# Attention and two expert layers on one core: the front of the kernel in a new order, with fewer operations on GpSimd

## The chip, the core and the metric

The kernel runs on one core of a Trainium2 chip. TensorE (PE in the profile) multiplies, VectorE (DVE), ScalarE (ACT) and GpSimd (POOL) work element by element, SyncE (SP) issues the transfers. The metric is the time of one execution in microseconds; lower is better. Most executions agree within 0.3%.

## What is computed

```python
# q, k, v: (2, 8, 576, 64); x: (1152, 512)
mask_plain = (rel >= 0) & (rel < 32)                       # heads 0 to 3
mask_dil = (rel >= 0) & (rel < 128) & (rel % 4 == 0)       # heads 4 to 7
scores = np.where(mask, scale * q @ k.T, -1e9)
attn = np.exp(scores - scores.max(-1, keepdims=True))
x = (attn / (attn.sum(-1, keepdims=True) + 1e-09)) @ v     # 1152 tokens of 512
h = x @ w_in                                               # (512, 1024)
e = np.exp(h - h.max(-1, keepdims=True))
solu = h * e / (e.sum(-1, keepdims=True) + 1e-9)
ln = (solu - mean(solu)) / np.sqrt(var(solu) + 1e-6) * g_ln
x = ln @ w_out                                             # (1024, 512)
p = domain_probs / (domain_probs.sum(-1, keepdims=True) + 1e-09)
for e in range(4):                                         # w1 (4, 512, 1024), w2 (4, 1024, 512)
    out += p[:, e:e + 1] * (np.maximum(x @ w1[e], 0.0) @ w2[e])
```

w_in and w_out arrive as 64-bit floats; everything else has 32 bits.

## The kernel before

**Precision.** A large product is made of three: each operand is split into a high part in the fp32r format and the rest, and high times high, high times low and low times high are added in PSUM. The splits are elementwise work: a copy that rounds (`copy`, on ACT, or on VectorE where the flag `alt` is set), and a subtraction for the low part (`tt` and `pick`, on GpSimd, or on VectorE with `alt`).

**Order by hand.** The first half of the kernel is not a loop. Each job is a generator that issues a few instructions and yields; the text `ORDER` names the jobs one after the other, and each mention advances that job by one step. A `+` behind a name sets `alt` for that step, `*n` puts n matmuls on a tile of zeros (`busy`, L178, the fillers) ahead of the step's own. Each engine does its instructions in the order in which the steps issue them. The jobs:

- lI, lO, lD, lP, lvd, lvp, lW: loads, issued on SP's queue.
- AD and AP: transposes of q and k (L290, L307), for the dilated and the plain heads.
- UD and UP, 12 units (`att_U`): mask and scores (L321, L332), maximum (L338), subtraction (L340), exponent on ACT (L343), sum (L345), plus 1e-9 (L347), reciprocal (L349), product into a padded buffer pd (L353), transposes (L359), copy pt, the product with v (L373), and the split of the result into xhi and xlo (L188 or L190, L275).
- VI and VO: decode of w_in and w_out from 64 to 32 bits (`convert`): the low word scaled on ACT (L204), the magnitude of the high word (L207 on VectorE or L209 on ACT), a clamp (L211), mask and shift (L213), the sign put back (L215), the sum of the two as integers (L217, GpSimd), then the split (L242; with the factor g_ln L258 to L266).
- H.t, 9 token tiles of 128: the first GEMM (24 matmuls of 128x512, L402) and the chain of softmax and normalisation (L407 to L425) with a power on GpSimd (L423).
- T.t: transposes of the result (L439) and their split (L188 or L190, L275 or L452). X.c.dp: the second GEMM, 48 matmuls of 128x384 (L465).
- XQ and WP: sums and splits of x and of the first w1 for a product with 7 instead of 8 multiplications (L496).

**The experts.** After ORDER come 8 half-experts in a loop. `up(0)` (512 tokens) and `up(1)` (640) are 7 products each (L578, 12 matmuls) with additions (L592 to L614), a relu on ACT (L588) and the low part on VectorE (L589). `down` is one step for each of 9 token tiles (L633, 12 matmuls), added to the result with the token's probability (L635, L637). For the first half-expert, `feed` puts the rest of XQ, the next w1 (WP.1) and w2 (WV) behind the products by the texts FIRST and SECOND. down 0 to 3 follow up(1), then up(0) of the next half-expert, then down 4 to 8.

**PSUM.** Two pools of two tiles each, pm and pa. `ptile` picks one by its argument and `alt`, `pair` takes them in turn.

Of the kernel before, what the change touches and what calls it, by code (L numbers as in the profile page):

```python
# [21 lines left out]
ORDER = """
lI.1 lD.0.0 lI.0 lP.0.0 AD.0.0*13 VI.1 VI.1 AD.0.0 VI.0 AP.0.0*24 lI.4 VI.1 lI.3 VI.0 VI.1 lI.2 VI.1 VI.0 lD.1.0
lP.1.0 VI.1 VI.0 AP.0.0 VI.4 VI.0 VI.0 VI.1 lvp.0.0 lO.0.0 VI.4+ VI.1 AD.0.0+*6 AP.0.0*8 VI.4 VI.4 VI.4 AP.0.0
UP.0.0+*6 VI.0+ AD.0.0 VI.3 UP.0.0 VI.0+ VI.4 VI.3 UP.0.0 UP.0.0 lO.0.1 VI.4 VI.3 VI.4 VI.2 VI.3 AD.1.0*30 UP.0.0 VI.3
AD.1.0 lD.0.1 AD.1.0*5 lvd.0 VI.2+ UP.0.0 AD.1.0 VI.3 VI.2 AP.1.0 AP.1.0 UD.0.0*9 UP.0.0 VI.3 VI.2 UP.0.0 lP.2.0 VI.2
UD.2.0 UD.0.0 UP.0.0+ UD.0.0 UD.0.0 UD.2.0 VO.0.0 UD.0.0 UD.1.0+ UP.0.0 UD.2.0 UD.0.0 VI.2 UD.0.0 UD.2.0 AP.1.0+
UD.0.0 AD.0.1+ VI.2+ AP.1.0 UP.0.0+ UD.2.0 VI.2 VO.0.1 UD.1.0 UD.2.0 AD.0.1 UD.1.0 lD.1.1 UD.0.0 UP.0.0 UD.1.0 UP.1.0
UD.2.0 UP.0.0 UD.2.0+ UD.0.0 UD.1.0 lvp.1.0 VO.0.1+ AD.0.1 VI.3 AD.0.1 UP.1.0 misc VO.0.0 UD.2.0+ VO.0.1 UD.1.0
AP.2.0+ UP.1.0 AP.2.0 UD.2.0 VO.0.1 UD.1.0 UD.0.0+ UD.1.0 lP.0.1 AP.2.0+ VO.0.1 AD.1.1+ VO.0.0 AP.2.0+ UP.1.0 UD.2.0+  # L30
AD.1.1 VO.0.1 VO.0.0 AD.1.1+ UP.2.0 UD.0.0 endE UD.2.0 VO.0.0 lO.1.1 UD.0.0 VO.0.1 lvp.2.0 VO.0.0 UP.1.0 UD.2.0 AD.1.1
UP.1.0 UD.1.0+ VO.0.1 UP.2.0 lO.1.0 VO.0.0+ AP.0.1 UP.1.0 UP.2.0 UD.1.1+ lP.1.1 UD.1.0 VO.0.0+ UP.2.0 UP.1.0 UP.2.0
AP.0.1 VO.1.1 UD.1.0+ UD.1.1 VO.1.1 UP.2.0 UP.1.0 UD.1.1 lvd.1 UD.0.1 VO.1.1 UD.1.0 UP.2.0 UD.1.1 UP.2.0 UP.1.0 VO.1.1
UD.1.0 UD.1.1 VO.1.0 AP.0.1+ UP.2.0 AP.0.1 VO.1.1 UD.1.1 AP.1.1+ VO.1.1 UP.2.0 UD.1.1 UD.2.1+ UD.0.1 AP.1.1 VO.1.0+
UD.0.1 VO.1.0 VO.1.0 VO.1.1+ UD.1.1 VO.1.0 lO.2.1 UP.1.0+ lP.2.1 UD.0.1 UD.1.1 UP.1.0 UD.2.1 UP.0.1 VO.1.0 UD.1.1
VO.1.1 UD.2.1 VO.1.0+ lO.2.0 UD.1.1 UP.1.0 UD.0.1 UD.2.1 AP.1.1+ UD.2.1 lvp.0.1 AP.1.1 UD.2.1 UP.2.0+ UD.1.1 UD.2.1
VO.1.0+ H.1 UP.2.0 UD.2.1 UD.0.1 VO.2.1 UD.1.1 VO.2.1 UD.0.1 UP.2.0 UD.0.1 VO.2.1 lvp.1.1 VO.2.1 UP.0.1 VO.2.0 VO.2.0
VO.2.1 UP.0.1 VO.2.1 VO.2.0 UP.0.1 VO.2.0 UP.0.1 VO.2.1 lO.3.1 UP.1.1 VO.2.0 H.1 VO.2.0 UD.2.1 UP.1.1 H.0 H.1 VO.2.1
lO.3.0 UP.0.1 UD.2.1 UP.1.1 UP.0.1 VO.3.1 H.1 UP.0.1 H.1 H.1 VO.3.1 VO.2.0+ VO.3.1 H.1 VO.3.1 UP.1.1 VO.2.0+ VO.3.0
UP.1.1 VO.3.0+ UD.2.1 H.0 UD.0.1 H.1 UD.2.1 UD.2.1 H.1 H.2 H.0 VO.3.1 H.1 UP.1.1 UD.0.1 H.0 H.0 VO.3.1 H.0 H.1+ H.0  # L40
UP.1.1 VO.3.0 VO.3.0 H.0 VO.3.0 VO.3.1 H.0 H.0 AP.2.1 UP.0.1 H.0 AP.2.1 UP.0.1 VO.3.0 VO.3.1+ T.0 T.0+ T.1 T.0 H.3 T.0
VO.3.0 T.1 T.1+ H.2 H.2 H.2 H.2 T.1 VO.3.0 H.2 UP.1.1 AP.2.1 AP.2.1 UP.0.1 H.2 UP.0.1+ lvp.2.1 UP.2.1*1 UP.0.1 UD.0.1
H.2 H.2 UD.0.1 UP.2.1 H.2 H.2+ UP.2.1 UD.0.1 UP.2.1 H.3 UP.1.1 T.2 UP.2.1 UP.1.1 H.4 T.2+ UP.2.1 H.3 H.3 UP.2.1 T.2+
H.3 H.3 T.2 H.3 H.3 UP.2.1+ UP.2.1 X.0.1 H.3 H.4 H.3 H.3 H.4 H.4 H.4 H.4 H.4 H.4 H.4 UP.2.1+ H.4 H.4+ UP.2.1 UP.1.1
UP.2.1+ UP.2.1 X.0.0 UP.1.1 UP.1.1 endA X.0.1+ T.3 X.0.0+ H.5 T.3 T.3 T.3 T.4 H.5 H.6 H.5 T.4+ H.5 T.4+ H.5 H.5 H.5
H.5 H.5 T.4 H.6 H.5 H.5+ T.5 H.6 H.6 H.6 H.6 T.5 H.6 H.7 H.6 T.5 H.6 T.5 H.6 H.6 H.7 H.7 T.6 H.7 H.8 H.7 H.7 T.6 H.7
T.6 H.7 T.6 H.7 X.1.0 H.7 H.8 H.8 H.7 H.8 H.8 H.8 H.8 H.8 H.8 H.8 H.8 T.7 T.7+ X.1.0+ T.7 T.8 X.1.1 T.7 T.8+ T.8+ T.8
endH lW.0 X.1.1 XQ.0 WP.0+ X.2.1 WP.0+ XQ.0+ WP.0 XQ.0+ XQ.0+ WP.0 XQ.0+ WP.0+ X.2.0 XQ.0+ X.2.1 WP.0 XQ.0+ WP.0+
WP.0+ XQ.0 WP.0 XQ.0 WP.0 XQ.0+ XQ.0+ XQ.0+ WP.0 XQ.0+ XQ.0 WP.0+ WP.0+ WP.0+ M X.2.0 XQ.0+ XQ.0 WP.0 M WP.0 WP.0+
WP.0+ M M M M M  # L50
"""
# [4 lines left out]

@with_exitstack
def fused_kernel(ctx, tc, q, k, v, w_in, w_out, g_ln, probs, w1, w2, out):
# [371 lines left out]
    def moe_T(t):  # L430
# [15 lines left out]
        if direct:  # L446
            lo_psum(ll[:, :, cols], pv, lh[:, :, cols])
        else:
            nc.scalar.copy(e, pa)
# [323 lines left out]
```

## Time and profile before

| | us |
|---|---|
| median of three runs | 590.05 |
| lowest, highest | 589.27, 590.79 |
| span of the profiled execution | 588.3 |
| TensorE busy in it | 549.9 (93%) |
| VectorE busy | 381.2 (65%) |
| ACT busy | 198.0 (34%) |
| GpSimd busy | 241.8 (41%) |

Of the profiled execution the span is known and no time of its own beside it. In the chain of work that ended last, 70% of the span is TensorE's and 16% VectorE's. A row of the profile says which line and engine, which operation, out<-in by the program's names, the shapes, how many, busy time and the mean of one in ns, and behind the last bar the idle time before them with what ended it.

### The profile page before, as it was taken

The numbers are of one execution on the slowest core, as the hardware profiler recorded it, in microseconds if no ns is written. First come the engines' busy times: TensorE is split into PE (matmuls) and PEld (weight loads), VectorE is DVE, ScalarE is ACT, GpSimd is POOL, SyncE is SP. The second block draws the span as 40 slices with busy tenths as digits, with TensorE's granted clock in tenths as the row PEclk, the third lists the DMA queues.
The fourth block names the chain that finished last, engine by engine and source line by source line (L and its number), as shares of the span: only waits on it lengthen the run. The fifth ranks groups of instructions, "written<-read, shape, count | busy, mean of one in ns | idle before, by whom it ended". The sixth has DMA issues, their size and how long they took to land.

```text
span 588.3 us, 9316 instructions
## 1 busy us (share of the span) xinstructions
PE 549.9 (93%) x3874; PEld 493.9 (84%) x3874; DVE 381.2 (65%) x506; ACT 198.0 (34%) x306; POOL 241.8 (41%) x178
## 2 busy tenths in 40 slices
...
GB/s 278 268 165 168 139 68 11 10 0 1 1 1 71 144 0 144 1 1 144 0 1 141 3 1 88 57 1 17 127 1 1 143 1 1 71 2 1 0 72 89
DMA packets 33945, 35.80 MB, mean 61 GB/s; under 512 B 18800, under 2 KB 21872, under 8 KB 33520
## 3 DMA queue, kind: packets, MB, share of 16 engines
...
## 4 chain that ended last, share of the span: by engine, by line
PE 70%; DVE 16%; issue 6%; POOL 3%; DMA 2%; ACT 2%; SPq 0%; POOLq 0%; ACTq 0%; DVEq 0%
PE pm L633 17%; PE pa L633 16%; PE pa L578 14%; PE pm L578 13%; PE pm L402 3%; PE pm L465 3%; DVE sw L496 2%; DMA draw<-in_moe_w_in_dram 1%; DVE cva L211 1%; DVE xol L496 1%; DVE lst L407 1%; DVE xlo L275 1%; DVE xoh L188 1%; DVE cva L215 1%; POOL hl L452 1%
## 5 line engine op out<-in xcount | busy, mean ns | idle before, releaser
L589 DVE SCALAR_TENSOR_TENSOR hl<-ct,hh 128x512 fp32r<-128x512 f32 (+1 forms) x64 | 68.4, 1088 | 37.0 <-ACT hh L588 37.0
L578 PE MATMUL pa<-xoh,hh 128*128 128x256 f32 (+1 forms) x192 | 57.8, 301 | 5.2 <-DVE ct L595 3.9
L578 PE MATMUL pm<-xoh,hh 128*128 128x256 f32 (+1 forms) x192 | 58.2, 303 | 4.2 <-DVE ct L595 2.8
L496 POOL TENSOR_TENSOR wl<-wl,wh 128x1024 fp32r<-128x1024 f32 x9 | 22.1, 2451 | 96.3 <-ACT wh L190 96.3
L633 PE MATMUL pm<-wh,hh 128*128 128x512 f32 (+1 forms) x152 | 58.4, 384 | 0.6 <-DVE xf L637 0.6
L588 ACT ACTIVATE hh<-ct 128x512 fp32r<-128x512 f32 (+1 forms) x64 | 42.3, 684 | 49.5 <-DVE ct L610 22.1
L633 PE MATMUL pm<-wl,hh 128*128 128x512 f32 (+1 forms) x152 | 58.3, 384 | 0.0
L633 PE MATMUL pm<-wh,hl 128*128 128x512 f32 (+1 forms) x152 | 58.3, 383 | 0.0
L578 PE MATMUL pm<-xol,hh 128*128 128x256 f32 (+1 forms) x192 | 57.7, 301 | 0.0
L578 PE MATMUL pm<-xoh,hl 128*128 128x256 f32 (+1 forms) x192 | 57.6, 300 | 0.0
L578 PE MATMUL pa<-xol,hh 128*128 128x256 f32 (+1 forms) x192 | 57.4, 299 | 0.0
L578 PE MATMUL pa<-xoh,hl 128*128 128x256 f32 (+1 forms) x192 | 57.3, 299 | 0.0
L633 PE MATMUL pa<-wh,hh 128*128 128x512 f32 x140 | 54.5, 389 | 0.0
L633 PE MATMUL pa<-wl,hh 128*128 128x512 f32 x140 | 54.5, 389 | 0.0
L633 PE MATMUL pa<-wh,hl 128*128 128x512 f32 x140 | 54.5, 389 | 0.0
L496 POOL TENSOR_TENSOR hl<-sw,hh 128x512 fp32r<-128x512 f32 x23 | 35.1, 1526 | 26.6 <-ACT hh L190 8.7
L637 DVE SCALAR_TENSOR_TENSOR xf<-pm,pr,xf 128x512 f32<-128x512 f32 (+1 forms) x33 | 24.1, 730 | 31.8 <-PE pm L633 31.8
L599 POOL TENSOR_TENSOR ct<-ct,ct 128x512 f32<-128x512 f32 (+1 forms) x16 | 23.7, 1481 | 47.9 <-ACT ct L598 46.5
L637 DVE SCALAR_TENSOR_TENSOR xf<-pa,pr,xf 128x512 f32<-128x512 f32 x31 | 23.1, 746 | 30.3 <-PE pa L633 30.3
L578 PEld LDWEIGHTS pa<-xoh,hh 128*128 128x128 f32 x192 | 36.9, 192 | 6.3 <-DVE ct L595 4.2
L578 PEld LDWEIGHTS pm<-xoh,hh 128*128 128x128 f32 x192 | 37.2, 194 | 5.1 <-DVE ct L595 3.0
L190 ACT CAST wh<-wl 128x1024 fp32r<-128x1024 f32 x16 | 16.8, 1054 | 70.7 <-PE pm L633 40.4
...
## 6 DMA issues: line engine op xcount, KB each, us to landing
...
```

The source lines that it names most:

```text
L188: nc.vector.tensor_copy(out, in_)
L190: nc.scalar.copy(out, in_)
L211: nc.vector.tensor_scalar(out=a, in0=a, scalar1=2.0 ** -15, scalar2=122879.9921875, op0=ALU.max, op1=ALU.min)
L402: nc.tensor.matmul(pm[:, n, :], lhsT=xx[:, kk, cols], rhs=ww["in", kk][:, 512 * n:512 * n + 512], start=(kk == 0 and i < 2), stop=(kk == K ...
L465: nc.tensor.matmul(pm[:, dd, 0:CW], lhsT=w_, rhs=x_[:, f, :], start=(f == 0 and i == 0), stop=(f == KF - 1 and i == 2))
L496: pick().tensor_tensor(out=out, in0=a, in1=b, op=op)
L578: nc.tensor.matmul(ps[:, ff, 0:n], lhsT=a[:, kk, fc], rhs=b[:, kk, :], start=kk == 0 and m == 0, stop=kk == 1 and m == 2)
L588: nc.scalar.activation(out=hv, in_=src, func=AF.Relu)
L589: nc.vector.scalar_tensor_tensor(out=lv, in0=src, scalar=0.0, in1=hv.bitcast(F32), op0=ALU.max, op1=ALU.subtract)
L599: nc.gpsimd.tensor_tensor(out=c12, in0=c21, in1=c22, op=ALU.add)
L633: nc.tensor.matmul(po[:, u, 0:dn], lhsT=h_[:, f, cols], rhs=w_, start=(f == 0 and i == 0), stop=(f == 3 and i == 2))
L637: nc.vector.scalar_tensor_tensor(out=acc[:, t, dc], in0=po[:, u, 0:dn], scalar=pr[:, t, e:e + 1], in1=acc[:, t, dc], op0=ALU.mult, op1=ALU ...
```

## The change

ORDER is written anew: no step has fillers, H.0 stands amid the attention units of the first batch, and the first half-expert is part of the text (u.0, u.1, d.0 to d.3, with the loads lV and lW and the steps of XQ.1, WP.1 and WV.0), so FIRST, SECOND and `feed` are gone. What else changes:

- `pick` gives VectorE where it gave GpSimd and the other way round, until `late` is set behind ORDER.
- `convert` takes the magnitude on ACT with a scale of 2^-112, which makes clamp and mask unnecessary; one shift and one sign operation remain on VectorE, and the integer sum goes by `pick`. w_out is always scaled on ACT and its low part made on VectorE.
- `att_U` has three sm and three pd buffers; column 64 of an sm buffer holds 1e-9, so that the sum contains it and L347 falls away.
- `moe_H` keeps maximum, exponent, product with its negative sum, and subtraction of the mean times 1024. What is a factor of a whole token (the softmax's sum, the normalisation) is left out and put into the probabilities `pr` once, in `scales` ("sc"). The sum of squares is made in `moe_T` on ACT; its low part always by VectorE out of PSUM.
- `ptile` chooses the PSUM pool by its argument alone, `pair` by a number that is passed; `up` and `down` are generators.

```diff
 def pick():
-        return nc.vector if alt[0] else nc.gpsimd
+        return nc.gpsimd if alt[0] != late[0] else nc.vector
...
-        pool, tag = (psm, "pm") if main != alt[0] else (psa, "pa")
+        pool, tag = (psm, "pm") if main else (psa, "pa")
...
-        if alt[0]:
-            nc.vector.tensor_scalar(out=au, in0=high.bitcast(U32), scalar1=0x7FFFFFFF, scalar2=None, op0=ALU.bitwise_and)
-        else:
-            nc.scalar.activation(out=a, in_=high.bitcast(F32), func=AF.Abs)
-        yield
-        nc.vector.tensor_scalar(out=a, in0=a, scalar1=2.0 ** -15, scalar2=122879.9921875, op0=ALU.max, op1=ALU.min)
-        yield
-        nc.vector.tensor_scalar(out=au, in0=au, scalar1=0x07FFFFFF, scalar2=3, op0=ALU.bitwise_and, op1=ALU.logical_shift_left)
...
-        nc.gpsimd.tensor_tensor(out=au, in0=au, in1=low.bitcast(U32), op=ALU.add)
+        nc.scalar.activation(out=a, in_=high.bitcast(F32), func=AF.Abs, scale=2.0 ** -112)
+        yield
+        nc.vector.tensor_scalar(out=au, in0=au, scalar1=3, scalar2=None, op0=ALU.logical_shift_left)
...
+        pick().tensor_tensor(out=au, in0=au, in1=low.bitcast(U32), op=ALU.add)
...
-        nc.vector.tensor_reduce(out=st[:, 1], in_=sm, axis=AX.X, op=ALU.add)
-        yield
-        nc.vector.tensor_scalar(out=st[:, 2], in0=st[:, 1], scalar1=1e-9, scalar2=None, op0=ALU.add)
+        nc.vector.tensor_reduce(out=st[:, 2], in_=smx, axis=AX.X, op=ALU.add)
...
+        nc.vector.scalar_tensor_tensor(out=e, in0=e, scalar=-1.0, in1=pm, op0=ALU.mult, op1=ALU.mult, accum_out=nsum[:, t:t + 1])
+        yield
+        if alt[0]:
+            nc.scalar.activation(out=e, in_=e, func=AF.Identity, bias=nsum[:, t:t + 1], scale=-float(DFF))
+        else:
+            nc.vector.tensor_scalar(out=e, in0=e, scalar1=-float(DFF), scalar2=nsum[:, t:t + 1], op0=ALU.mult, op1=ALU.add)
...
+        nc.scalar.activation(out=e, in_=e, func=AF.Square, accum_out=esq[:, t:t + 1])
...
+    def scales():
+        nc.vector.tensor_scalar(out=esum, in0=esum, scalar1=1e-9, scalar2=None, op0=ALU.add)
+        nc.vector.reciprocal(out=nmx, in_=esum)
+        nc.vector.scalar_tensor_tensor(out=esq, in0=esq, scalar=1.0 / DFF ** 3, in1=nmx, op0=ALU.mult, op1=ALU.mult)
+        nc.vector.tensor_tensor(out=esq, in0=esq, in1=nmx, op=ALU.mult)
+        nc.vector.tensor_scalar(out=esq, in0=esq, scalar1=1e-6, scalar2=None, op0=ALU.add)
+        nc.gpsimd.tensor_tensor(out=esq, in0=esq, in1=mhalf, op=ALU.pow)
+        nc.vector.scalar_tensor_tensor(out=nmx, in0=nmx, scalar=1.0 / DFF, in1=esq, op0=ALU.mult, op1=ALU.mult)
+        nc.vector.tensor_tensor(out=pr, in0=pr, in1=nmx.unsqueeze(2).to_broadcast([128, NTT, E]), op=ALU.mult)
```

VectorE's queue before, early in the front, where two tiles of w_in (eva, cva) are decoded while the first unit of attention (sm_340, st_341) runs:

```order
L340 TENSOR_TENSOR sm_340<-pm_301,st_341 128x384
L211 TENSOR_SCALAR eva_338<-eva_338 128x1024
L213 TENSOR_SCALAR eva_338<-eva_338 128x1024
L345 TENSOR_REDUCE st_341<-sm_340 128x6
L215 SCALAR_TENSOR_TENSOR eva_338<-draw3_239,eva_338 128x1024
L207 TENSOR_SCALAR cva_162<-draw2_243 128x1024
L347 TENSOR_SCALAR st_341<-st_341 128x6
L211 TENSOR_SCALAR cva_162<-cva_162 128x1024
L349 RECIPROCAL st_341<-st_341 128x6
L213 TENSOR_SCALAR cva_162<-cva_162 128x1024
```

VectorE's queue now, at the same place, with the units sm0 and sm1 (L326 is the maximum, L328 the subtraction, L333 the sum, L202 the shift, L204 the sign, L231 the low part of w_in, L182 `copy`, L337 the product into pd):

```order
L202 TENSOR_SCALAR eva_323<-eva_323 128x1024
L333 TENSOR_REDUCE st_363<-sm0_112 128x6
L326 TENSOR_REDUCE st_443<-pa_382 128x6
L326 TENSOR_REDUCE st_449<-pa_414 128x6
L231 TENSOR_TENSOR wl0_199<-cva_174,wh0_198 128x512
L328 TENSOR_TENSOR sm1_113<-pa_414,st_449 128x6x64
L333 TENSOR_REDUCE st_352<-sm2_114 128x6
L182 COPY qTp_369<-pm_370 128x2x2x96
L204 SCALAR_TENSOR_TENSOR eva_323<-draw1_272,eva_323 128x1024
L335 RECIPROCAL st_363<-st_363 128x6
L337 TENSOR_TENSOR pd0_109<-sm0_112,st_363 128x6x64
```

Of a decode, two operations are left between those of attention; the low part, a copy out of PSUM and the product into pd have come in.

VectorE's queue before, in up(1) of the first half-expert (L595 to L614 the additions, L589 the low parts, L496 sums of the next w1, L635 the first two down steps):

```order
L595 TENSOR_TENSOR ct1_2297<-pa_2314,ct0_2296 128x640
L496 TENSOR_TENSOR sw1_2291<-sw0_2290,wh6_2147 128x2x256
L602 TENSOR_TENSOR ct0_2296<-pa_2347,ct0_2296 128x640
L589 SCALAR_TENSOR_TENSOR hl1_2142<-ct0_2296,hh1_2141 128x2x320
L606 TENSOR_TENSOR ct1_2297<-pm_2367,ct1_2297 128x640
L496 TENSOR_TENSOR sw2_2292<-wh6_2147 128x2x256
L610 TENSOR_TENSOR ct3_2299<-pa_2385,ct3_2299 128x640
L589 SCALAR_TENSOR_TENSOR hl1_2142<-ct3_2299,hh1_2141 128x2x320
L614 TENSOR_TENSOR ct1_2297<-pm_2403,ct1_2297 128x640
L589 SCALAR_TENSOR_TENSOR hl1_2142<-ct1_2297,hh1_2141 128x2x320
L589 SCALAR_TENSOR_TENSOR hl1_2142<-ct2_2298,hh1_2141 128x2x320
L635 TENSOR_SCALAR xf_1652<-pa_2433,pr_76 128x512
```

VectorE's queue now, in u.1 (L566 to L594 the additions, L558 the low parts, L464 sums and low parts of x and w1, L618 the down steps):

```order
L566 TENSOR_TENSOR ct1_2110<-pm_2127,ct0_2109 128x640
L464 TENSOR_TENSOR xol_1790<-xf_1433,xoh_1789 128x2x320
L464 TENSOR_TENSOR sw3_1964<-xf_1433,sw1_1962 128x640
L618 TENSOR_SCALAR xf_1433<-pm_2156,pr_76 128x512
L182 CAST xoh_1789<-sw3_1964 128x2x320
L464 TENSOR_TENSOR xol_1790<-sw3_1964,xoh_1789 128x2x320
L576 TENSOR_TENSOR ct0_2109<-pm_2171,ct0_2109 128x640
L558 SCALAR_TENSOR_TENSOR hl1_1974<-ct0_2109,hh1_1973 128x2x320
L464 TENSOR_TENSOR hl_1799<-wh6_1937,hh_1798 128x512
L582 TENSOR_TENSOR ct1_2110<-pa_2209,ct1_2110 128x640
L618 TENSOR_SCALAR xf_1433<-pa_2196,pr_76 128x512
L584 TENSOR_TENSOR ct2_2111<-ct1_2110,ct2_2111 128x640
```

The first down steps stand between the products of u.1, and some low parts of x and w1 and one of the additions have come over from GpSimd.

## Rows read from the trace of the kernel before

**Rows 1.** Stretches of the span: engines busy (instructions), PEclk, DMA share, GB/s.

```profile
0.00:112.30 112.30, 89.99 (x1191) 74.17 (x1191) 94.38 (x171) 67.83 (x109) 58.76 (x63) 0.91 0.57 145
8.00:50.00 42.00, 33.49 (x540) 28.48 (x539) 36.17 (x54) 23.09 (x37) 24.91 (x15) 0.80 0.87 210
50.00:92.60 42.60, 35.16 (x481) 28.68 (x481) 40.54 (x82) 31.21 (x55) 19.73 (x19) 0.99 0.47 124
112.30:193.00 80.70, 79.15 (x467) 74.33 (x465) 43.34 (x69) 19.79 (x29) 20.40 (x16) 1.00 0.04 14
193.00:243.20 50.20, 39.41 (x219) 35.85 (x219) 43.91 (x41) 18.41 (x28) 38.98 (x23) 0.90 0.26 85
243.20:588.30 345.10, 341.38 (x2005) 309.55 (x2003) 199.61 (x227) 91.95 (x140) 123.71 (x77) 1.00 0.12 41
```

**Rows 2.** VectorE's instructions by line and form, 0 to 112.3 us.

```profile
L211 DVE TENSOR_SCALAR cva<-cva 128x512 f32<-128x512 f32 x10 | 8.7, 872 | 1.3 <-ACT cva L209 1.3
L213 DVE TENSOR_SCALAR cva<-cva 128x512 uint32<-128x512 uint32 x10 | 7.7, 770 | 0.2
...
L347 DVE TENSOR_SCALAR st<-st 128x6 f32<-128x6 f32 x12 | 6.3, 522 | 0.0
...
L215 DVE SCALAR_TENSOR_TENSOR cva<-cvr,cva 128x512 uint32<-128x512 uint32 x8 | 5.5, 688 | 0.1
...
L353 DVE TENSOR_TENSOR pd<-sm,st 128x384 f32<-128x384 f32 x2 | 2.4, 1185 | 0.0
...
L207 DVE TENSOR_SCALAR cva<-cvr 128x512 uint32<-128x512 uint32 x3 | 1.9, 630 | 0.0
...
L417 DVE TENSOR_SCALAR lst<-lst 128x1 f32<-128x1 f32 x4 | 0.6, 152 | 0.1
...
L188 DVE COPY kTp<-pa 128x384 f32<-128x384 f32 x1 | 0.6, 564 | 0.0
```

**Rows 3.** Timeline of the front: start, duration (us), engine, line.

```profile
25.98 2.77 POOL L217 TENSOR_TENSOR eva<-eva,draw 128x1024 uint32<-128x1024 uint32 x1 [1.16 <-DVE eva L215]
...
26.43 2.35 DVE L347 TENSOR_SCALAR st<-st 128x6 f32<-128x6 f32 x1
...
34.45 0.16 DVE L347 TENSOR_SCALAR st<-st 128x6 f32<-128x6 f32 x1
...
60.34 0.43 DVE L213 TENSOR_SCALAR cva<-cva 128x512 uint32<-128x512 uint32 x1
```

**Rows 4.** GpSimd's integer sums by form, 0 to 112.3 us.

```profile
L217 POOL TENSOR_TENSOR cva<-cva,cvr 128x512 uint32<-128x512 uint32 x8 | 10.6, 1319 | 7.9 <-DVE cva L215 3.0 <-ACT wh L261 1.9 <-ACT xhi L190 1.6
```

**Rows 5.** The chain that ended last: start, duration (us), TensorE's groups.

```profile
112.52 8.33 PE pm L465 x48
...
243.22 1.42 PE pa L578 x12
...
253.17 2.73 PE pm L633 x12
...
266.78 1.76 PE pa L578 x12
```

**Rows 6.** TensorE's waits, 193 to 243.2 us: total, times, longest.

```profile
PE pa L578 <- DVE ct L595: 3.9, 1, 3.9
```

**Rows 7.** VectorE's L589 of 128x512: 193 to 243.2 us, then 243.2 to 588.3.

```profile
L589 DVE SCALAR_TENSOR_TENSOR hl<-ct,hh 128x512 fp32r<-128x512 f32 x4 | 5.8, 1476 | 2.2 <-ACT hh L588 2.2
...
L589 DVE SCALAR_TENSOR_TENSOR hl<-ct,hh 128x512 fp32r<-128x512 f32 x28 | 18.8, 690 | 14.7 <-ACT hh L588 14.7
```

**Rows 8.** The fillers L178 alone, by stretch (TensorE busy, PEld busy, PEclk).

```profile
30.00:50.00 20.00, 0.00 (x0) 0.00 (x0) 0.73 0.70 127
...
sum 60.00, PE 15.29 PEld 11.90; mean PE 3.06 PEld 2.38
```

**Rows 9.** Timeline: a score tile of pa, its matmuls and its maximum.

```profile
70.87 0.34 PE L321 MATMUL pa<-mask,identb 128*128 128x192 bf16 x2
...
75.10 0.54 DVE L338 TENSOR_REDUCE st<-pa 128x6 f32<-128x384 f32 x1
```

More of the change, by code (lines that the diff above doesn't have):

```diff
@@ L28 @@
[L28 to L37, printed above, removed]
@@ L102, in fused_kernel @@
     vd = ap1.tile([128, 3, 4, 2 * D], F32, name="vd", tag="vd")
-    pds = []
-    for i in range(2):
-        pds.append(ap1.tile([128, 2, 480], F32, name=f"pd{i}", tag=f"pd{i}"))
+    pds = [ap1.tile([128, 2, 480], F32, name=f"pd{i}", tag=f"pd{i}") for i in range(3)]
+    sms = [ap1.tile([128, 6, 65], F32, name=f"sm{i}", tag=f"sm{i}") for i in range(3)]
     warmb = ap1.tile([128, 224], BF16, name="warmb", tag="warmb")
@@ L311, in att_AP @@
                 yield
+    unit = {}
+    for b in range(B):
+        for quad, t in (("D", 0), ("P", 0), ("D", 1), ("D", 2), ("P", 1), ("P", 2)):
+            unit[quad, t, b] = len(unit)
     def att_U(quad, t, b):
@@ L444, in moe_T @@
         yield
-        direct = not alt[0]
[L446 to L449, printed above, removed]
-        yield
-        if not direct:
-            nc.gpsimd.tensor_tensor(out=ll[:, :, cols], in0=e.rearrange("p u (f t) -> p (u f) t", t=128), in1=lh[:, :, cols].bitcast(F32),
-                                    op=ALU.subtract)
+        lo_psum(ll[:, :, cols], pv, lh[:, :, cols])
     def moe_X(c, dp):
```

212 lines of the change are left out of this document (99 added, 113 removed).

## The prediction

> **What bounds the kernel now.** I read the table of stretches first [rows 1]. It cuts the span of 588.3 us into three parts. The front, 0 to 112.3 us, is attention, the decode of both weight matrices and the first five H steps; it ends where the second GEMM's first step, X.0.0, starts. There VectorE is busy 94.38 of 112.3 us and GpSimd 58.76, and TensorE shows 89.99 at a mean granted clock of 0.91. Look at 50 to 92.6: VectorE 40.54 of 42.6 us, DMA share 0.47. That is an engine at its limit. Before 50 us it shares the limit with the loads (DMA share 0.87). The middle, 112.3 to 193, is TensorE at 79.15 of 80.7 us with a clock of 1.00: nothing to gain. In the first experts, 193 to 243.2, TensorE works 39.41 of 50.2 us, VectorE 43.91 and GpSimd 38.98. After 243.2 TensorE is busy 341.38 of 345.1 us; the instructions there are the same on both sides.
>
> The first experts show who is late: the list of TensorE's waits names VectorE's adds L595 first [rows 6]. These stand in VectorE's queue behind work that runs slower than it needs to: the split L589 of 128x512 takes 1476 ns there and 690 ns later [rows 7]. The same shows in the front. The addition of 1e-9 to six numbers (L347) took 0.16 us with GpSimd quiet and 2.35 us while GpSimd added 1024 integers (L217) [rows 3]. So GpSimd's work is paid twice, on GpSimd and as stretched work on VectorE.
>
> How much is that in all? Repricing VectorE's rows at the shortest duration of the same form gives about 18 us of stretch in the front and 16.6 in the first experts: L347 at a mean of 522 ns against 160, L213 at 770 against 430 [rows 2, 3], L589 at 1476 against 690, and so on over all forms. That is about 0.35 us of VectorE for each us of GpSimd elementwise work in the front (52 us without the masks of the setup) and 16.6/38.98 = 0.43 in the first experts.
>
> **The change, part by part.** Sums are made against the span of 588.3; the median of 590.05 lies 1.75 us above, which I leave as it is.
>
> *Front, taken from VectorE.* The clamp L211, 8.7 us for ten of 512 words and 2.1 for three of 1024: 10.8. The sign mask L207, five in all: 3.0. L347, 6.3. Four one-column steps of each of the four softmax chains in this part, 16 at 152 ns: 2.4 [rows 2]. Sum 22.5 us.
>
> *Front, put on VectorE.* Integer adds (L217), two of them: no row of before has one on VectorE, so I bound them by L215 of 512 words at 688 ns and by GpSimd's own 1319 [rows 2, 4]; I take the lower, since the other integer form on VectorE lies there: 1.9 us for one of 512 and one of 1024 words, 3.8 at most. Splits of the decoded weights by the form of L215: 2.3 for w_out, 1.9 for w_in. Copies out of PSUM that ACT did: seven query or key tiles and three of xhi at 564 ns [rows 2] or in proportion to their size, and one pt, 7.3 in all. Two more products L353, 0.55 (as a copy of that size) to 1185 ns [rows 2], low end because GpSimd is quieter: 1.1. Setup of a third pair of buffers 1.2. Sum 15.7 us, up to 19.
>
> *Front, stretch.* GpSimd keeps about 28 of its 52 us. What stays on VectorE carries about 8.5 us of the 18 (the rest went with L211, L207 and L347); at 28/52 it is 4.8, so 3.7 less, and I add 2 for new operations that can be held. VectorE's work falls by 22.5 - 15.7 + 1.7 = 8.5 us, with bounds of 3 and 13. The chain of a token tile through the softmax is six steps shorter and loses its visit to GpSimd, and the products no longer wait for a handoff; VectorE's idle 17.9 us falls by perhaps 3. X.0.0 moves forward by about **11 us** (8 to 15). ACT gains w_in's absolute value with its scale and the Square of each tile, and drops as many copies; it was busy 67.83 of 112.3 [rows 1], which covers that. The fillers cost nothing and give back nothing by themselves: 15.29 us of matmuls, all but one in the first 30 us [rows 8], while the DMAs were still bringing inputs.
>
> *Middle.* An X step is 48 matmuls in 8.33 us [rows 5], and TensorE was full. The transposes' lows move from GpSimd to VectorE, which had 37 us free there; the per-token factors are seven short operations that meet nobody before the first down step. Nothing, from -1.5 to +2. SP's queue: the loads of w1 and w2 are issued in the order text rather than behind it, under X steps; the load of the first half-expert has more matmuls ahead of its use than before.
>
> *First experts.* Fourteen products (7 at 1.42, 7 at 1.76) and four down steps at 2.73 are 33.2 us of TensorE [rows 5], against 50.2. Before, the four downs came last, after the waits; now d.0 to d.3 stand between the products of u.1 and fill what these wait for. VectorE needed 43.91 - 16.6 = 27.3 us unstretched and takes over about 2.5 from GpSimd: 29.8. GpSimd falls from 23 instructions of 1.69 us [rows 1] to about 11, 18 us, so the stretch is 16.6 x 18/39 = 7.7. VectorE then needs 37.5 us and stays the later engine, with 1.5 of idle 39 us: **11 us** less (8 to 14; 17 if TensorE's 33.2 is reached).
>
> On that stretch, rows 3 and 7 say only that operations of VectorE stretch while GpSimd runs. The Trainium skill, "SBUF — State Buffer", section "Who interferes with whom", says it is an exclusive lock on a shared port pair, taken by an operation with two SBUF inputs or one in a two-port mode, and that an operation with at most one SBUF input outside those modes is not held. L347 with its one small input was held for 2.35 us, so the trace agrees only if it runs in such a mode. By the rule the new copies out of PSUM are not held at all, I would drop the 2 us added for them and more of the rest, and the sum would come to about 564 as an estimate.
>
> *Afterwards.* The PSUM pools now alternate by a fixed parity and repeat a pool at the seams; the tile that is reused was read two products earlier, and I cost it at nothing. If that cover is gone, up to 0.7 us at each of 14 seams, 10 us.
>
> Sum: 590.05 - 11 - 11 = **568**.
>
> **The rivals.**
> *Both floors are met.* If the stretch goes with GpSimd's work and VectorE is no longer last anywhere, X.0.0 starts at about 93 us (loads to 40 us, then TensorE's remaining work) and the first experts take 33.2: 590.05 - 19 - 17 = 554. For it: 17 us of VectorE stretch in a stage of 50. Against: VectorE keeps 29.8 us of real work there.
> *VectorE is refilled.* The 15.7 us put on it come at the stretched prices (19 and more), and the order spends the rest in handoffs: the front gains nothing, the experts 11: 579. For it: 40.54 of 42.6 busy. Against: the six-number and clamp rows go for certain.
> *One PSUM pool holds attention.* Before, 13 of the 36 score, transpose and value tiles of attention went to the pool pm; now every score, transpose and value tile takes one of the two buffers of pa, 45 tiles with AP's and T's. Of before, a score tile was held from 70.87 us until after its row at 75.10 and a subtraction, 6.3 us [rows 9], a transposed one about 1.8 us. At a mean of 4 us two buffers pass 45 tiles in 90 us, under the new front of 101; at 4.7 the gain of the front is gone: 579. For it: queues on VectorE lengthen exactly this hold. Against: they shorten here.
> *The clock, on the slow side.* Without fillers attention's small matmuls stand alone until H.0. With them it was granted 0.73 between 30 and 50 us [rows 8], so part of that stretch ran at 1.2 GHz. TensorE's 90 us less 15.3 of fillers at 0.91 are about 68 us at 2.4 GHz and 136 at 1.2. If it stays low until H.4, X.0.0 comes at about 130, 18 us late: 590.05 + 18 - 11 = 597. It decides from a mean clock of 0.55 in the front, where 68 us become 123 and eat the experts' gain. Against: no filler stands in 30 to 92.6 us, and the clock there went from 0.73 to 0.99 without one, on H's matmuls, which now start earlier [rows 1, 8]. The Trainium skill, "TensorE: Matmul & The Clock Gate", section "What's actually happening", has the throttled state as the default and activity as what releases it; that speaks for this rival in the first 20 us alone, where the loads bound the front anyway.
>
> **How the numbers follow.** Forecast 568: 0.57, with its own range 560 to 576 from the bounds of the two gains. Both floors (554): 0.18. VectorE refilled (579): 0.10. The PSUM pool (579): 0.10. The clock (597): 0.05. The range must leave out no more than 0.2: 553 to 581 leaves out the clock and the tails of the floors. Faster by over 0.3% (about 1.8 us, what a measurement of this kernel can tell from no change): all but the clock and a little, 0.94; within 0.3%: 0.02; slower: 0.04, the clock without its mild end.
>
> **What would show it.** Right, if in the new profile X.0.0 starts near 101 us, VectorE is busy some 8 us less before it, L589 in the first experts falls towards 0.9 us, and from u.0 to the second up(0) is some 39 us with TensorE's last waits still on VectorE. Wrong, if TensorE waits for score tiles of pa, if its granted clock before X.0.0 lies under 0.8, if the integer adds on VectorE take over 1.3 us for 512 words, or if a half-expert afterwards takes more than 46.8 us, which the same fourteen products and nine downs take now.

## The result and the profile after

| | before | after |
|---|---|---|
| median, us | 589.66 | 572.59 |
| lowest, highest | 588.81, 590.79 | 571.59, 573.67 |
| profiled execution, its span | – | 572.3, 570.5 |

Measured beside each other, the changed kernel takes 0.9712 of the time of the one before (95% interval 0.9692 to 0.9732): 17 us less. The forecast was 568, with a range of its own of 560 to 576.

The same stretches as in [rows 1], cut at the same events: the start of X.0.0, of u.0, of the second up(0), the end. Columns are the length, then TensorE, weight loads, VectorE, ACT and GpSimd busy with instruction counts, granted clock, DMA share, GB/s.

```profile
0.00:102.36 102.36, 78.41 (x1088) 63.24 (x1089) 83.43 (x146) 61.13 (x97) 33.66 (x45) 0.95 0.59 159
102.36:181.66 79.30, 79.10 (x467) 74.34 (x466) 47.64 (x62) 24.98 (x39) 11.18 (x7) 1.00 0.04 14
181.66:224.11 42.45, 35.71 (x218) 32.71 (x217) 39.72 (x43) 15.76 (x25) 19.73 (x11) 0.96 0.28 100
224.11:570.50 346.39, 342.68 (x2004) 310.62 (x2004) 202.66 (x232) 93.11 (x142) 127.06 (x79) 1.00 0.12 41
```

Against [rows 1] the front is 9.9 us shorter (112.30 to 102.36), the middle 1.4 (80.70 to 79.30), the first experts 7.8 (50.20 to 42.45), and the rest 1.3 longer (345.10 to 346.39). That is the 17.8 us of span.

The front by 20 us, the last row to X.0.0:

```profile
20.00:40.00 20.00, 14.13 (x261) 10.92 (x260) 16.79 (x33) 11.93 (x18) 6.91 (x5) 0.74 0.94 239
40.00:60.00 20.00, 15.70 (x252) 12.42 (x257) 19.89 (x26) 9.07 (x15) 8.34 (x5) 1.00 0.41 101
60.00:80.00 20.00, 18.27 (x270) 14.86 (x262) 17.39 (x33) 14.51 (x26) 3.70 (x4) 1.00 0.55 163
80.00:102.36 22.36, 20.87 (x188) 17.77 (x187) 20.34 (x32) 18.14 (x31) 7.43 (x7) 1.00 0.28 82
```

VectorE, fourth in each row, has 0.1 us free between 40 and 60 us. From 60 us on TensorE is the fuller one, 18.27 of 20 and 20.87 of 22.36. Before, VectorE was the fuller one over the whole of 50 to 92.6 us [rows 1]. The chain of work that ended last says the same: from 36.3 to 59.5 us it runs almost without a break on VectorE, and 37.3 of the 43 us from 59.59 to the second GEMM are TensorE's. The place where it passes over, in the changed kernel (start, duration):

```profile
58.97 0.57 DVE xlo L256
59.54 0.05 issue
59.59 0.34 PE pa L307 x2
```

In the first experts, VectorE by form. The low price of L589 of 128x512, 690 ns [rows 7], is reached again (L558); the sums and subtractions L464 with their inputs in SBUF are mostly far above their best:

```profile
L464 DVE TENSOR_TENSOR sw<-xf,sw 128x640 f32<-128x640 f32 x2 | 4.0, 2004 | 0.0
L464 DVE TENSOR_TENSOR sw<-xf 128x640 f32<-128x640 f32 x2 | 3.9, 1950 | 0.0
L464 DVE TENSOR_TENSOR xol<-xf,xoh 128x1280 fp32r<-128x1280 f32 x1 | 3.7, 3654 | 0.0
L464 DVE TENSOR_TENSOR xol<-sw,xoh 128x640 fp32r<-128x640 f32 x3 | 3.4, 1144 | 0.2 <-ACT xoh L184 0.2
L558 DVE SCALAR_TENSOR_TENSOR hl<-ct,hh 128x512 fp32r<-128x512 f32 x4 | 2.7, 687 | 1.4 <-ACT hh L556 1.4
...
L464 DVE TENSOR_TENSOR xol<-xf,xoh 128x640 fp32r<-128x640 f32 x1 | 0.8, 817 | 0.0
```

The costliest single meeting, from the timeline of VectorE, GpSimd and TensorE. GpSimd's low part of w2 begins at 187.43 us; VectorE's low part of x, which begins behind it, takes 3.65 us, and the addition L566, which frees the tile that TensorE's next product needs, stands behind both:

```profile
187.43 2.77 POOL L464 TENSOR_TENSOR wl<-wl,wh 128x1024 fp32r<-128x1024 f32 x1
...
187.89 3.65 DVE L464 TENSOR_TENSOR xol<-xf,xoh 128x1280 fp32r<-128x1280 f32 x1
...
191.47 0.68 DVE L566 TENSOR_TENSOR ct<-pm,ct 128x512 f32<-128x512 f32 x1
...
192.21 0.39 PE L545 MATMUL pm<-xoh,hh 128*128 128x256 f32 x1 [3.19 <-DVE ct L566]
```

### The profile page after: what moved, and what is told of

It is laid out like the page before. It is cut to its first block, busy times and chain, and to the rows that moved or that the text cites. A ratio compares the mean times of both kernels' runs of the same rounds, so it can differ in the third digit from the quotient of the medians.

```text
span 570.5 us, 9019 instructions
## 1 busy us (share of the span) xinstructions
PE 535.9 (94%) x3772; PEld 480.9 (84%) x3772; DVE 373.4 (65%) x480; ACT 195.0 (34%) x302; POOL 191.6 (34%) x142
## 4 chain that ended last, share of the span: by engine, by line
PE 80%; DVE 11%; issue 3%; POOL 2%; DMA 2%; ACT 2%; SPq 1%; DVEq 0%; POOLq 0%; ACTq 0%
PE pm L615 16%; PE pa L615 16%; PE pm L545 14%; PE pa L545 14%; PE pm L386 8%; PE pm L433 6%; DMA rdq<-in_q_dram 2%; DVE xol L464 1%; PE pa L413 1%; DVE sw L464 1%; PE pa L357 1%; PE pa L318 1%; DVE xlo L256 1%; PE pa L343 1%; PE pm L271 1%
## 5 line engine op out<-in xcount | busy, mean ns | idle before, releaser
L558 DVE SCALAR_TENSOR_TENSOR hl<-ct,hh 128x512 fp32r<-128x512 f32 (+1 forms) x64 | 62.0, 987 | 34.8 <-ACT hh L556 34.8
L615 PE MATMUL pm<-wh,hh 128*128 128x512 f32 (+1 forms) x148 | 56.9, 384 | 0.6 <-DVE xf L620 0.6
L615 PE MATMUL pm<-wl,hh 128*128 128x512 f32 (+1 forms) x148 | 56.8, 384 | 0.0
L615 PE MATMUL pm<-wh,hl 128*128 128x512 f32 (+1 forms) x148 | 56.7, 383 | 0.0
L615 PE MATMUL pa<-wl,hh 128*128 128x512 f32 x144 | 56.1, 390 | 0.0
L615 PE MATMUL pa<-wh,hh 128*128 128x512 f32 x144 | 56.1, 390 | 0.0
L615 PE MATMUL pa<-wh,hl 128*128 128x512 f32 x144 | 56.0, 389 | 0.0
L464 POOL TENSOR_TENSOR wl<-wl,wh 128x1024 fp32r<-128x1024 f32 x9 | 22.1, 2452 | 98.6 <-ACT wh L184 98.5
L464 POOL TENSOR_TENSOR hl<-sw,hh 128x512 fp32r<-128x512 f32 x20 | 30.2, 1508 | 32.7 <-ACT hh L184 27.3
L464 POOL TENSOR_TENSOR hl<-rw,hh 128x512 fp32r<-128x512 f32 x11 | 18.2, 1655 | 65.9 <-ACT hh L184 65.9
```

The costliest lines, as they stand in the source:

```text
L464: pick().tensor_tensor(out=out, in0=a, in1=b, op=op)
L558: nc.vector.scalar_tensor_tensor(out=lv, in0=src, scalar=0.0, in1=hv.bitcast(F32), op0=ALU.max, op1=ALU.subtract)
L615: nc.tensor.matmul(po[:, u, 0:dn], lhsT=h_[:, f, cols], rhs=w_, start=(f == 0 and i == 0), stop=(f == 3 and i == 2))
```

## The experiments

The time of the kernel before was 588.8 to 590.6 beside the runs below; each is told by its own median, its ratio where it matters, and by the three events, X.0.0, u.0 and the second up(0).

### The decode alone

```diff
-        if alt[0]:
-            nc.vector.tensor_scalar(out=au, in0=high.bitcast(U32), scalar1=0x7FFFFFFF, scalar2=None, op0=ALU.bitwise_and)
-        else:
-            nc.scalar.activation(out=a, in_=high.bitcast(F32), func=AF.Abs)
+        nc.scalar.activation(out=a, in_=high.bitcast(F32), func=AF.Abs, scale=2.0 ** -112)
         yield
-        nc.vector.tensor_scalar(out=a, in0=a, scalar1=2.0 ** -15, scalar2=122879.9921875, op0=ALU.max, op1=ALU.min)
         yield
-        nc.vector.tensor_scalar(out=au, in0=au, scalar1=0x07FFFFFF, scalar2=3, op0=ALU.bitwise_and, op1=ALU.logical_shift_left)
+        nc.vector.tensor_scalar(out=au, in0=au, scalar1=3, scalar2=None, op0=ALU.logical_shift_left)
...
```

The operation that puts the sign back stays and takes one bit instead of two.

> The kernel before with nothing changed but the decode: the magnitude with its scale on ACT, no clamp and no mask on VectorE (13 operations, 10.8 us, and five of L207, 3.0 us, go; ACT gains five). Theory (VectorE's work bounds the front): X.0.0 starts 5 to 9 us earlier than at 112.3 us, the time is 581 to 585. Rival (VectorE's queue is refilled by waits on GpSimd and ACT, the order sets the front): X.0.0 moves by less than 2 us, 588 to 590.

582.65 us, ratio 0.9907 (0.9875 to 0.9938). The stretch up to X.0.0, then the first experts:

```profile
0.00:104.73 104.73, 86.11 (x1190) 71.19 (x1191) 85.53 (x153) 70.72 (x114) 58.41 (x63) 0.97 0.61 155
...
185.38:235.34 49.96, 39.28 (x217) 35.70 (x217) 43.78 (x41) 18.41 (x28) 38.85 (x23) 0.90 0.24 85
```

X.0.0 comes 7.6 us earlier (by the medians the kernel gains 6.4), VectorE has 8.8 us less work, GpSimd's 58.41 us are those of before [rows 1], and the order is the old one. In the old kernel, the decode alone gives most of what the whole change gives in the front. The granted clock of the front rose too, from 0.91 to 0.97, and what that gave is not separated. The first experts, 49.96 us, are as before.

### No fillers

Every `*n` in the old ORDER is left out: 102 fillers by the text and by the trace, one less than the expectation counts.

> The kernel before without its 103 fillers and nothing else. Theory (the loads and VectorE bound the front while the fillers run): within 1 us of 590. Rival (fillers keep TensorE's clock up): X.0.0 starts 4 us later or more, with a mean granted clock before it clearly under 0.91. Second rival (the fillers stood in the way of attention's matmuls): 2 to 6 us faster.

590.57 us, ratio 1.0024 (1.0005 to 1.0042): 1.5 us slower by the medians. The stretch up to X.0.0:

```profile
0.00:113.17 113.17, 81.35 (x1088) 66.40 (x1089) 98.13 (x171) 68.30 (x109) 58.48 (x63) 0.95 0.56 144
```

X.0.0 comes 0.9 us later, yet the mean granted clock before it is 0.95, higher than the 0.91 with fillers. A higher mean clock is not what the fillers gave. VectorE's same 171 instructions took 98.13 us instead of 94.38; whether that made the 0.9 us was not tried.

### The clamp back

```diff
-        nc.scalar.activation(out=a, in_=high.bitcast(F32), func=AF.Abs, scale=2.0 ** -112)
+        nc.scalar.activation(out=a, in_=high.bitcast(F32), func=AF.Abs)
         yield
-        nc.vector.tensor_scalar(out=au, in0=au, scalar1=3, scalar2=None, op0=ALU.logical_shift_left)
+        nc.vector.tensor_scalar(out=a, in0=a, scalar1=2.0 ** -15, scalar2=122879.9921875, op0=ALU.max, op1=ALU.min)
+        nc.vector.tensor_scalar(out=au, in0=au, scalar1=0x07FFFFFF, scalar2=3, op0=ALU.bitwise_and, op1=ALU.logical_shift_left)
...
```

> The changed kernel with the old decode's clamp and mask in the same step as its shift: 13 operations more on VectorE in the front, 0.58 us of 512 words and 0.69 of 1024 where nothing stretches them, 7.9 us, 10.8 at the stretched prices of before. Theory (VectorE's work bounds the front): X.0.0 starts 5 to 10 us later than at 102.4, time 578 to 583. Rival (the front is held by the PSUM pool pa and by the order, VectorE has 18.9 us idle there): under 2 us, 573 to 575.

578.08 us, 5.5 more than the changed kernel: the lower end of what the theory wanted. X.0.0 stands at 106.66, 4.3 us later, a little less than the 5 that it wanted, with 4.8 us more work on VectorE. VectorE's clamp in this kernel's front, by form, and the front from 40 to 50 us:

```profile
L202 DVE TENSOR_SCALAR cva<-cva 128x512 f32<-128x512 f32 x10 | 5.3, 530 | 8.0 <-ACT cva L200 8.0
...
40.00:50.00 10.00, 9.01 (x64) 7.46 (x63) 8.34 (x11) 4.13 (x8) 2.40 (x1) 0.50 0.75 198
```

The clamp takes 530 ns in the changed front and took 872 before [rows 2]: for ten of them 3.4 us, beside the 5.3 of the operations themselves. The 4.3 us are not VectorE's alone. In this execution TensorE was granted 0.50 of full speed, 1.2 GHz, from 30 to 50 us (the changed kernel had 0.53 from 30 to 40 and 1.00 from 40 to 50), and from 39.4 to 49.2 us the chain of work that ended last is TensorE's but for 1.8 us. The low clock does not explain the time by itself: two other executions with a higher mean clock over their span, 0.982 against 0.976, took 577.73 and 580.93 us, this one 576.96.

### The downs last

d.0 to d.3 in ORDER are moved behind the last product of u.1.

> The changed kernel with d.0 to d.3 behind the last product of u.1 in ORDER, where they stood before. Theory of the prediction (the downs fill TensorE's waits): u.0 to the second up(0) grows from 42.4 us by 4 to 8, time 576 to 581. Rival (VectorE, 39.7 of 42.4 us busy, bounds the stage wherever the downs stand): under 2 us, 573 to 575.

576.22 us, 3.6 more. From u.0 to the second up(0):

```profile
182.25:227.47 45.22, 37.99 (x218) 34.11 (x217) 42.62 (x45) 17.09 (x26) 21.85 (x12) 0.92 0.28 94
```

The first experts grow by 2.8 us (42.45 to 45.22), between the two expectations. Standing between the products is worth 2.8 of the 7.8 us won there. Of these 2.8 us, 2.3 are TensorE's own busy time, 37.99 against 35.71 for the same 218 matmuls, at a granted clock of 0.92 instead of 0.96. The rest of the 7.8 was not split further; the counts tell a part of it: VectorE and GpSimd had 41 and 23 instructions in that stretch before [rows 1] and have 43 and 11 in the changed kernel, ten fewer, while the stretch behind it has seven more (227 and 77 before, 232 and 79 now).

### Elementwise work back on GpSimd in the front

```diff
-        return nc.gpsimd if alt[0] != late[0] else nc.vector
+        return nc.gpsimd if front[0] or alt[0] != late[0] else nc.vector
```

`front` holds until the end of H.

> The changed kernel with every operation that `pick` places put back on GpSimd until the end of H: nine that VectorE does in the front (four products into pd, 2.3 us, two integer sums, 2.8, three low parts of w_in, 2.9; 8.0 us) move over. Theory of the prediction (work on GpSimd stretches VectorE by some 0.35 us for each us, here 13 us or so, 4.5): VectorE falls by 3 to 4 us, handoffs take most of that back, X.0.0 within 2 us of 102.4, time 571 to 575. Rival (what left GpSimd in the front carried the gain): X.0.0 later by 4 us or more, 577 and up. Second rival (VectorE's busy time alone counts, no stretch): X.0.0 earlier by 5, under 568.

573.48 us, ratio 0.9734 (0.9709 to 0.9759), not told apart from the changed kernel. The stretch up to X.0.0:

```profile
0.00:102.07 102.07, 76.31 (x1089) 61.49 (x1089) 75.75 (x138) 61.09 (x97) 45.90 (x54) 0.95 0.61 159
```

VectorE's 83.43 us fall to 75.75 and GpSimd's 33.66 rise to 45.90, and X.0.0 stands at 102.07. So what `pick` had moved off GpSimd in the front did not carry the gain. One price of the expectation failed: 12.2 us more on GpSimd should have stretched VectorE by some 4.5, yet VectorE lost 7.7 of the 8.0 us that moved. In this kernel's chain of work that ended last, GpSimd's operations have come in for VectorE's, five of them with 7.9 us up to 50 us where the changed kernel has one of 2.8, and the chain passes over to TensorE at nearly the same time (start, duration):

```profile
43.55 2.08 issue
45.63 2.42 POOL eva L207
...
59.27 0.34 PE pa L308 x2
```

By the chain, what VectorE was rid of came back as waits for GpSimd.

### The low parts of x on GpSimd in the first experts

```diff
-        tt(lo, src, hi.bitcast(F32), ALU.subtract)
+        (eng or pick()).tensor_tensor(out=lo, in0=src, in1=hi.bitcast(F32), op=ALU.subtract)
...
+        eng = nc.gpsimd if s else None        # in prep_x, passed to its splits
```

> The changed kernel with the five low parts of XQ.1 that VectorE makes in the first experts (7.9 us there) put on GpSimd, which is busy 19.7 of 42.4 us. Theory of the prediction (0.43 us of stretch for each us of GpSimd, here 9.3): VectorE falls by 4, GpSimd has room: from u.0 to the second up(0) 40 to 43 us, time 570 to 573. Rival (GpSimd is slow and its results come late, TensorE waits for xol): 45 us or more, 575 and up.

569.58 us, ratio 0.9672 (0.965 to 0.9694). From u.0 to the second up(0):

```profile
181.49:221.15 39.66, 34.31 (x218) 31.22 (x217) 35.65 (x37) 15.94 (x25) 30.84 (x16) 1.00 0.31 107
```

VectorE falls by 4.1 us as expected, the stretch to 39.66 us, 2.8 less than in the changed kernel. Of the 2.8, 1.4 are TensorE's busy time (34.31 against 35.71), at a granted clock of 1.00 instead of 0.96. The ratio's interval just touches the changed kernel's (0.9692 to 0.9732); the stretch is clearer, since the four runs above and below whose first experts are unchanged (the clamp back, the work back on GpSimd, both runs with transposed tiles) have 42.0 to 42.4. Five operations more on GpSimd make it faster: here VectorE is the late engine, and what it gives away counts more than what GpSimd's work costs it.

### The addition first

Two neighbouring names of ORDER are exchanged (XQ.1 and u.0), so that L566 no longer stands behind the 3.65 us.

> The changed kernel with one pair of ORDER names exchanged: the addition L566 of u.0 is issued ahead of the low part of XQ.1 (128x1280, 3.65 us held beside GpSimd's low part of w2) instead of behind it. Theory (VectorE's whole work bounds the stage, a shorter wait here comes back at the next product): the 3.19 us wait goes, less than 1.5 us of it remains as a gain, 571 to 573. Rival (the one queue position costs its wait and the low clock behind it): 4 to 5 us less, 567 to 569.

572.66 us. The changed kernel's waits of TensorE from 181.6 to 224.1 us (total, times, longest), and below it those of this kernel from 178 to 226:

```profile
PE pm L545 <- DVE ct L566: 4.5, 2, 3.2
PE pa L545 <- DVE ct L594: 2.3, 1, 2.3
```

```profile
PE pa L545 <- DVE ct L582: 3.8, 1, 3.8
PE pa L545 <- DVE ct L594: 1.7, 1, 1.7
```

The wait of 3.19 us went and one of 3.8 came at a later product; all waits together fell from 6.8 to 5.5. The stretch is 42.01 us instead of 42.45. One queue position was not the cause; that VectorE's work as a whole is late fits this and VectorE's 39.24 busy of 42.01 us.

### Pools in turn

```diff
-        k = g % 2 + (1 if s else 0 if g else 1)
+        k = g % 2 + 1
```

> The changed kernel with the PSUM pools strictly in turn at every seam of the half-experts (up(0) from the second half-expert on starts in the other pool). Prediction (repeating a pool costs nothing): within 0.5 us of 572.6. Rival (the repeat cost the 2.3 us wait of the second up(0) on L594, and the 1.2 us that the rest became longer): 1.5 to 3.5 us less, 569 to 571, and 345.2 us after the start of the second up(0).

571.65 us, ratio 0.9709, not told apart. TensorE's wait at the seam, of the changed kernel and, in the next block, of this one:

```profile
PE pa L545 <- DVE ct L594: 2.3, 1, 2.3
```

```profile
PE pa L545 <- DVE ct L594: 0.8, 1, 0.8
```

This kernel from u.0 to the second up(0), and from there to the end:

```profile
184.44:224.44 40.00, 35.53 (x218) 32.85 (x217) 37.47 (x40) 14.43 (x23) 19.73 (x11) 0.96 0.31 106
224.44:571.80 347.36, 342.82 (x2005) 310.61 (x2003) 205.07 (x235) 94.29 (x144) 126.95 (x79) 1.00 0.12 41
```

The first experts and the rest together take 387.36 us instead of 388.84. So the repeated pool cost 1.5 us at one seam of the profiled execution, where VectorE reads the last tile late. TensorE's 342.8 us of work afterwards stay at the changed kernel's value and not at 341.5 as before, so the parity is not what made the rest longer. (The profiled execution of this run had its loads later than others, X.0.0 at 105.10; only what follows u.0 is used.)

### Transposed tiles in the other pool

```diff
-        tp = ptile(False)
+        tp = ptile(True)
```

> The changed kernel with the 12 transposed tiles of attention in the pool pm instead of pa, which then passes 33 tiles instead of 45 in the front. Rival of the prediction (the two buffers of pa hold attention back; TensorE waits some 9 us in the front for reads of pa tiles by VectorE): X.0.0 starts 3 us earlier than at 102.4 or more, 567 to 570. Theory (VectorE until 60 us, then TensorE, 18.3 and 18.5 of each 20 us, bound the front): within 1.5 us, 571 to 574; later where H's tiles in pm are held up.

584.4 us, X.0.0 at 111.09. In pm the transposed tiles meet those of H and of AD and AP; TensorE's longest waits up to 114 us:

```profile
PE pm L343 <- ACT pt L184: 6.7, 3, 4.9
PE pm L343 <- DVE pt L182: 4.4, 1, 4.4
```

That tells little of pa, since it trades one pool for a fuller one. A smaller step has `tp = ptile(b == 0)`, six tiles of the first batch:

> The changed kernel with the transposed tiles of the first batch alone (6 of 12) in the pool pm, where few of H's tiles stand yet; a cleaner trial of the PSUM rival than all 12, whose tiles had to wait for H's and copies pt in pm (X.0.0 at 111.1 us). Rival of the prediction (the two buffers of pa hold the first 60 us back): X.0.0 2 to 4 us earlier than at 102.4, 568 to 571. Theory (VectorE bounds 30 to 60 us, 10.0 and 9.9 of 10 us busy from 40 to 60): within 1.5 us of it, 571 to 574.

572.12 us, ratio 0.9708 (0.9667 to 0.975). The stretch up to X.0.0:

```profile
0.00:102.09 102.09, 79.00 (x1088) 64.11 (x1089) 82.92 (x147) 60.92 (x97) 33.62 (x45) 0.93 0.60 159
```

X.0.0 stands at 102.09 against 102.36, with pa relieved of six tiles by 60 us. This trial is not clean either. TensorE's waits on score tiles of pa in the changed kernel's front, and in the next block TensorE's longest waits in this one's from 20 us on:

```profile
PE pa L343 <- DVE sm L328: 4.0, 3, 2.4
```

```profile
PE pm L343 <- ACT pt L184: 4.9, 1, 4.9
PE pm L343 <- DVE qTp L182: 2.3, 1, 2.3
```

The waits on pa are gone and waits on pm stand in their place. What speaks against pa is the changed kernel itself: all but 0.2 us of the 4.0 lie before 40 us, and behind them VectorE has 0.1 us free up to 60 us, so an earlier tile would have found it busy.

### Two more steps on the first experts

The low parts of x on GpSimd and the pools in turn together; then also the second low part of w2 by VectorE (the last `WV.0+` becomes `WV.0`).

> The changed kernel with the five low parts of XQ.1 on GpSimd and the PSUM pools in turn at the seams, both as tried alone (39.7 us from u.0 to the second up(0), and a seam wait of 0.8 instead of 2.3 us). Theory (both waits stand on VectorE's lateness at the end of u.1, which the first edit has already taken away): 0 to 0.7 us less than the first alone, 568.5 to 570. Rival (the gains add): 1.5 us or more less, 567 to 568.

> As the run before it, and the second low part of w2 (128x1024), which TensorE's first down step waited for by 2.2 us on GpSimd, on VectorE. Theory (GpSimd's queue is the late one there): that wait goes, 1 to 2 us less, 567 to 568.5. Rival (VectorE, 35.7 of 39.7 us busy, becomes late again in u.1): no gain or a loss, 569 to 572.

568.44 us (0.9659, 0.9624 to 0.9694) and 568.06 us (0.9645, 0.9609 to 0.9682). The first experts of the one and of the other:

```profile
180.97:220.41 39.44, 34.16 (x218) 31.37 (x217) 35.43 (x37) 15.81 (x24) 30.85 (x16) 1.00 0.33 107
```

```profile
181.66:220.03 38.37, 34.15 (x217) 31.32 (x217) 34.35 (x38) 15.82 (x24) 28.09 (x15) 1.00 0.32 110
```

TensorE's wait on the low part of w2, in the one and in the other:

```profile
PE pm L616 <- POOL wl L469: 2.2, 1, 2.2
```

```profile
PE pm L616 <- DVE wl L469: 1.1, 1, 1.1
```

Half of that wait went; the expectation had all of it. Neither step is told apart from the run before it by its time; both together with the first are: 0.9645 lies below the changed kernel's 0.9712 with intervals that do not touch, 4.5 us by the medians. This is the fastest version tried.

## Why the prediction came out

**The front, 11 us forecast, 9.9 measured.** The step held, and its largest term was the right one. Taking clamp and mask away alone gives 7.6 us in the old kernel. VectorE's work fell by 10.9 us, inside the bounds of 3 and 13 and above the 8.5 taken. (In the sum for the stretch, 28/52 of 8.5 is 4.6 and not 4.8; it moves nothing.) For copies out of PSUM and other new operations I had added 2 us of stretch. Three of these copies ran while GpSimd worked, pt at 34.29 us (945 ns), xhi at 36.28 (0.56 us) and kTp at 43.66 (0.55), and without it they take no less: xhi 0.56 us at 73.12, kTp 0.54 at 33.29, and pt's 768 columns lie on the line of qTp's 384 (549 ns) and qTd's 576 (745), which met none. The Trainium skill ("SBUF — State Buffer", "Who interferes with whom") says that operations with at most one input in SBUF, outside the two-port modes, are not held; for these three the trace sides with it over my 2 us. The integer sum on VectorE took 683 ns for 512 words, the low bound, and 2119 for 1024 beside GpSimd, above the 1.2 that I took. VectorE's idle did not fall by 3 us; it rose from 17.9 to 18.9. The rows by 20 us and the chain show where: from 60 us on TensorE is over nine tenths busy, and VectorE's time there is free for waiting. Up to 60 us it is still VectorE that is full. That the gain stopped short of 11 us because TensorE was next is what this suggests; no run took work off TensorE in the changed kernel's front to show it. I had put TensorE's limit at 93 us.

**The middle, 0 forecast, 1.4 won.** TensorE had 1.5 us idle before and 0.2 after. Inside the bound of -1.5.

**The first experts, 11 forecast, 7.8 measured.** This is the term that was mis-sized. I had VectorE at 29.8 us of work, 7.7 of stretch and 1.5 idle, 39 in all. At the best price of each form in the trace it is 28.7 of work, 11.1 of stretch and 2.7 idle, 42.5 in all: the stretch is 3.4 us over, the idle 1.2, the work 1.1 under. The stretch was scaled by GpSimd's busy time, 19/39 of 16.6. GpSimd's time came out as forecast (19.7 against 18), but what it meets on VectorE now are low parts and sums with two inputs in SBUF. An addition out of PSUM beside GpSimd was not held; L582 of 128x640 took 0.82, as without it:

```profile
215.06 1.51 POOL L464 TENSOR_TENSOR hl<-sw,hh 128x512 fp32r<-128x512 f32 x1 [3.29 <-ACT hh L184]
...
215.33 0.82 DVE L582 TENSOR_TENSOR ct<-pa,ct 128x640 f32<-128x640 f32 x1
```

So the price of a microsecond of GpSimd is not one number (0.43 before, 0.56 now, next to nothing for what was put back in the front); it depends on what stands on VectorE at that moment. One thing the sum left out: TensorE's matmuls there took 39.41 us before and 35.71 now for the same number of them, at a granted clock of 0.90 and 0.96. That is 3.7 of the 7.8 us. The clock fell right behind the 3.19 us wait, to 0.62 from 192.2 to 196.7 us, so fewer waits may pay a second time through it. How much of the 3.7 would have been hidden behind VectorE was not tried.

**The seams, 0 forecast.** The cover was thinner than I said: a tile read two products earlier is free only if VectorE is not late. At the end of u.1 it is, and the repeated pool cost 1.5 us there. (The time of the trial was not told apart from the changed kernel's; the 1.5 us are the profiled execution's.)

**The rest, 0 forecast, 1.3 lost.** The same matmuls run a little slower: the chain shows most of the 49 products of 256 columns at 1.44 instead of 1.42 us (up to 1.0) and thirteen down steps at 2.75 instead of 2.72 (0.4). Every variant of the changed kernel has it, none of the old one, and the pools are not its cause. The cause stays open. That 1.3 us were lost here and 1.4 won in the middle, neither forecast, is luck: the two cancel, and the 4.6 us by which the time missed 568 are about the 1.1 us of the front and the 3.2 of the first experts.

**The rivals.** The clock: without fillers the old kernel has a higher mean clock before X.0.0, 0.95. In the variants with the same front it was 0.93 to 1.00 while X.0.0 stayed between 101.6 and 102.8 us (one execution with late loads aside), and the one with 1.00 came at 102.61, no sooner than the others. The Trainium skill ("TensorE: Matmul & The Clock Gate", "What's actually happening") has the throttled state as the default and says that activity releases it. A throttled stretch did occur, 0.53 of full speed from 30 to 40 us, so mostly 1.2 of 2.4 GHz, behind ten microseconds with TensorE busy 7.32 us; it did not delay X.0.0, since the variant with 1.00 there was as late. With the clamp back, though, a longer one stood on the chain. In the whole kernel the clock may have helped the change: of the 35 executions of the kernel before that were made beside the experiments, the 16 with a mean clock of 0.977 and more took 588.6 us on average and the 11 with 0.971 and less 590.6. The changed kernel's four have 0.985 to 0.988. Carried on, that would be some 3 us of the 17, an estimate; whether the higher clock is a cause there or follows from fewer waits was not separated.

The PSUM pool: relieving pa won nothing, though its trial moved waits into pm; the reason to set it aside is that VectorE was full behind these waits. VectorE refilled: no, its work fell. Both floors: the front came to 102.4 instead of 93, the experts to 42.5 instead of 33.2; the best variant reaches 38.4.

**The signs.** X.0.0 (102.4 for 101), VectorE's work before it (10.9 us less for 8) and the low parts (0.69 us for 0.9) came as signs of being right; the first experts came at 42.5 instead of 39, with the last waits on VectorE as said. Of the signs of being wrong, two came in a mild form and did not decide: TensorE did wait for score tiles of pa, 4.0 us in all, and a half-expert afterwards takes about 47.0 us instead of 46.8 (1.3 us over seven of them). The clock before X.0.0 was 0.95, not under 0.8, and the integer sum of 512 words took 0.68 us, not 1.3.
